# Regrouping the 64x64 products of a chunked recurrence into three runs, with ScalarE's order written out by hand

## The chip, the cores and the metric

One Trainium2 chip, one of its cores. The time is device time in microseconds (us) from launch to end, the median of several executions; lower is better. A profile is taken from one further execution of its own. The core has five instruction queues that run side by side and meet at semaphores: TensorE (PE in the profile; PEld is its weight load), VectorE (DVE), ScalarE (ACT), GpSimd (POOL) and SyncE (SP), which only issues DMAs here. GpSimd and ScalarE issue DMAs too.

## What is computed

Two blocks behind each other. The first is a recurrence over 768 tokens, for 4 batches x 8 heads with a 40x40 state each:

```python
for t in range(S):
    y[:, :, t] = np.einsum('bhd,bhde->bhe', rt, state)
    Sa = np.einsum('bhde,bhe->bhd', state, at)
    state_decay = state * wt[:, :, None, :] - np.einsum('bhd,bhe->bhde', Sa, bt)
    state = state_decay + np.einsum('bhd,bhe->bhde', vt, kt)
```

The second is a feed-forward block on the 3072 x 320 outcome:

```python
h = x @ w_in                                   # 320 -> 1024
e = np.exp(h - h.max(-1)); solu = h * e / (e.sum(-1) + 1e-9)
ln = (solu - mean(solu)) / np.sqrt(var(solu) + 1e-6) * g_ln
return ln @ w_out                              # 1024 -> 320
```

## The kernel before

The recurrence is worked off in chunks of 64 tokens, two batches at a time: 24 chunk pairs, numbered i, even and odd ones for the two batch pairs. Within a chunk the recurrence becomes matrix algebra with small products, one for each head: of 64x64 or less, 16 units to a step, that is 32 matmul instructions, since a product of float32 takes two. Four of them sit in the four quarters of TensorE's array. What the recurrence makes implicit is the inverse of a triangular 64x64 matrix for each head. The two 32x32 diagonal blocks of two chunks' heads are inverted together on VectorE (`invert`), the coupling of the blocks on TensorE (`couple`, `close`).

One pass of the main loop (line 785), called a slot here, does a bit of everything in a software pipeline. With i the slot's number, it solves and reads chunk i, prepares chunk i+1, makes decays and norms for chunk j = i+5, and does the feed-forward of chunks i-3 and i-4 (`m-2`, `m-3` with m = i-1). The stages, by the names of the tiles in the profile:

- `decay(i)` (L310): Ln of w on ScalarE (`lw`), a running sum on TensorE (`pcum`), two Exp (`ei`, `inv`). `decay_turned`: transposes `pei`, copied to `ex` by ScalarE.
- `front(i)`: transposes `pa` and `pb`; VectorE makes `aT`, ScalarE copies `bT`. `scaled` makes `kb` on GpSimd.
- `norm(i)`: products `pnt`, masked by VectorE into `nt` (L362), stored to DRAM (`nt_dram`, L388).
- `invert(n)` (L402): n counts pairs of chunks. `spread` loads the blocks back with four DMAs (`blk`, L399), then come 30 steps of VectorE, each a product and a subtraction (L415, L417); the first step begins with memsets (L407) and reads `blk` (L409). The outcome goes to `uu_dram`, from where `bring(i)` loads `tu` and `uh` on SP for each chunk.
- `flip`, `couple`: VectorE transposes `tu`, TensorE makes `py`, ScalarE copies it to `wy`. `close`: `pz`, copied into `tu`.
- `attend_kv`, `attend_rs`: transposes `pk`, `pv`, `pr` and of the state `pst`, copied by ScalarE to `kT`, `vT`, `rT`, `s`. `by_value` copies v and r on GpSimd for them. `scores`: products `ps` (two lots), masked to `psi` and `lv`.
- `carried`, `driven`: products `px`, copied to `x0`. `solved`: products `pu`, copied to `nuT` and `lu`. `answered`: `pl`, masked into `lu`.
- `read(i, own)`: `pyo`, outputs and state update, in two halves with a fence (a drain of TensorE) between. `leave(i)`: VectorE makes `x` (L604) and `tot` (L619) of it, GpSimd the new state; SP, and `left` on GpSimd, move `x` to `xT`.
- `hidden` (`h`, two matmuls of 512 columns each for full width, and two of half the rows), `exped` (maximum on VectorE, L655, Exp on ScalarE, L658), `weighed` (L664), `spreadof` (statistics, then a power on GpSimd, `rs`, L681), `folded` (transposes `plnT`), `output` (`po`, 16 matmuls in two lots, then `osb` and its store).

In the first slots `narrow` also converts the 64-bit weights, on VectorE and ScalarE, and `mean_begun` and `centred` take the mean out of the output weights.

The order of TensorE, VectorE, GpSimd and SP is the program's order, written by hand (line 87). ScalarE's order is left to the scheduler. The inverse is a Python generator: `some(n)` takes n steps off a list of begun inverses, and goes on in the next when one is used up. Where the steps stand between the other VectorE work is set by the four numbers of `shares`/`pieces` in each slot. An inverse is begun, and its `blk` loads issued, in slots where j is odd, so in even slots.

PSUM is used through three pools: `ps1` with two tiles of two banks each (`banks`: px, pu, pnt, pl, ps, py, pz, pyo in turn, eight in a slot), `ps2` with one tile of two banks (`h`), and `ps3` with two tiles of one bank (`bank`: transposes, pcum, po). A tile of a pool is used again when all readers of its last contents are done.

Of the kernel before, what the change touches and what calls it, by code (L numbers as in the profile page):

```python
# [48 lines left out]
def kernel(  # L49
# [37 lines left out]
    ctx.enter_context(tc.manual_schedule(engines={mybir.EngineType.PE, mybir.EngineType.Pool,  # L87
                                                 mybir.EngineType.DVE, mybir.EngineType.SP}))
# [85 lines left out]
    def split(dst, bits, c):  # L174
        n, width = dst.shape
        word = bits.bitcast(I32).rearrange("p (n two) -> p n two", two=2)
        hi, low16 = word[:, :, 1], bits.bitcast(U16).rearrange("p (n four) -> p n four", four=4)[:, :, 1]
        scale = two.tile([P, 512], I32, tag="scale", name="scale", bufs=1)[0:n, 0:width]
        ts, act, stt = nc.vector.tensor_scalar, nc.scalar.activation, nc.vector.scalar_tensor_tensor
        man = dst.bitcast(I32)  # L180

        ts(out=scale, in0=hi, scalar1=20, scalar2=0x7FF, op0=ALU.logical_shift_right, op1=ALU.bitwise_and)
        ts(out=man, in0=hi, scalar1=0xFFFFF, scalar2=None, op0=ALU.bitwise_and)
        act(out=scale, in_=scale, func=AF.Relu, scale=-1.0, bias=top[:, 0:1])
        act(out=scale, in_=scale, func=AF.Relu, scale=-2.0 ** 23, bias=top[:, 1:2])
        if c is None:
            g36 = 2.0 ** -36
            act(out=dst, in_=man, func=AF.Copy, scale=2.0 ** -20, bias=1.0)
        else:
            g, g20, g36 = (x[:, c:c + 1] for x in g_cols)  # L190
            act(out=dst, in_=man, func=AF.Identity, scale=g20, bias=g)
        yield
        stt(out=hi, in0=hi, scalar=-2 ** 31, in1=scale, op0=ALU.bitwise_and, op1=ALU.bitwise_or)
        stt(out=dst, in0=low16, scalar=g36, in1=dst, op0=ALU.mult, op1=ALU.add)
        nc.vector.tensor_tensor(out=dst, in0=dst, in1=hi.bitcast(FP32), op=ALU.mult)

    def narrow(n, n_steps=0):

        for x in range(n):
            load, part = next(parts)  # L200
            rest = split(*part)
            next(rest)
            some(n_steps // n + (x < n_steps % n))
            for _ in rest:
                pass

            if part is landed[load][-1] and load in LANDS_NEXT:
                land(LANDS_NEXT[load], nc.gpsimd)
        if not n:
            some(n_steps)  # L210
# [42 lines left out]
    def mm(o, lhsT, rhs, start=True, stop=True):  # L253
        nc.tensor.matmul(o, lhsT=lhsT, rhs=rhs, start=start, stop=stop, skip_group_check=True)  # L254

# [53 lines left out]

    def decay(i):  # L310
        if not ok(i):
            return
        d = st[i]
        lw = two.tile([P, DM], FP32, tag="lw", name="lw", bufs=1)
        nc.scalar.activation(out=lw, in_=d["raw_w"].rearrange("p h d -> p (h d)"), func=AF.Ln)
        t = (bank("pcum") if i > 5 else ps2.tile([P, DFF], FP32, tag="h", name="h"))[:, 0:DM]
        nc.tensor.matmul(t, lhsT=c_("cum"), rhs=lw, start=True, stop=True)
        nc.scalar.activation(out=ei_t[0][:, :, 0:D], in_=heads(t), func=AF.Exp)
        inv = d["inv"] = two.tile([P, DM], FP32, tag="inv", name="inv", bufs=4)
        nc.scalar.activation(out=inv, in_=t, func=AF.Exp, scale=-1.0)  # L320
# [31 lines left out]
    def front(i):  # L352
        if not ok(i):
            return
        d = st[i]
        t = turned("a", d["raw_a"])
        aT = d["aT"] = tokens("aT", AHEAD)
        nc.vector.tensor_tensor(out=aT[0:W2], in0=t, in1=d["ex"][0:W2, :, :, 0:C], op=ALU.mult)
        d["bT"] = kept("bT", turned("b", d["kb"][:, H:]))
# [33 lines left out]
    def spread(n):  # L393
        nb = two.tile([P, Q, Q], FP32, tag="blk", name="blk")
        for y in range(2):
            for e in range(2):
                home = C * y + Q * e
                queue = nc.gpsimd if n > 1 or y and not n else nc.sync
                queue.dma_start(out=nb[home:home + Q], in_=blocks[n][:, Q * e:Q * e + Q, Q * e:Q * e + Q])  # L399
# [77 lines left out]
    def attend_rs(i):  # L477
# [4 lines left out]
        d["rT"] = kept("rT", turned("r", r_t[0]), 2)  # L482
        if ci:
# [4 lines left out]
            d["s"] = two.tile([P, 4, P], FP32, tag="s", name="s")  # L488
# [36 lines left out]
    def driven(i):  # L525
# [3 lines left out]
        if d["opened"]:  # L529
            fence()  # L530
# [38 lines left out]
    def read(i, own):  # L569
# [14 lines left out]
        else:  # L584
            fence()
# [52 lines left out]
    def hidden(i, some):  # L638
# [4 lines left out]
        for kt, x in some:  # L643
            if (kt, x) == (0, 0):
# [3 lines left out]
               start=kt == 0, stop=kt == NK - 1)  # L648

    def exped(i):  # L650
# [3 lines left out]
        nmax = small.tile([P, 1], FP32, tag="nmax", name="nmax")  # L654
        nc.vector.tensor_reduce(out=nmax, in_=d["h"], axis=AX.X, op=ALU.max, negate=True)  # L655
        e = d["e"] = two.tile([P, DFF], FP32, tag="e", name="e", bufs=1)
        d["esum"] = small.tile([P, 1], FP32, tag="esum", name="esum")
        nc.scalar.activation(out=e, in_=d["h"], func=AF.Exp, bias=nmax, accum_out=d["esum"])  # L658
# [74 lines left out]
    for n in range(3):  # L733
        land(n, nc.sync)
    decay(0)
    decay_turned(0)
    for i in range(4):
# [4 lines left out]
        front(i)  # L742
        decay(i + 1)
        norm(i)
        decay_turned(i + 1)
        if i == 0:
            load_keys(2, "ba")
        if i == 1:
# [5 lines left out]
            load_keys(4, "w")  # L754
            some(8)
        if i == 2:
            load_values(0)
            load_keys(1, "k")
            some(8)
    load_keys(5, "w")  # L760
    load_keys(4, "ba")
    begin_inverse(1)
    for i in (2, 3):
        load_keys(i, "k", nc.gpsimd)
    by_value(0)
    scaled(2, "k")
    load_keys(4, "k", nc.gpsimd)
    scaled(3, "k")
    scaled(4)
    decay(5)  # L770
    load_keys(6, "w")
    land(3, nc.sync)
    some(14)
    load_keys(5, "ba")
# [3 lines left out]
    load_keys(5, "k")  # L778
    for n in (4, len(lands)):
        land(n, nc.sync)  # L780


    shares = {-1: (0, 6, 2, 6), 0: (0, 6, 4, 6), 1: (0, 6, 3, 6), 2: (0, 6, 3, 6), 3: (0, 6, 3, 6)}
    narrowed = {-1: (0, 1), 0: (1, 1), 1: (1, 2), 2: (1, 2), 3: (1, 1)}
    for i in range(-1, N + 3 + LAG):
        j, m = i + AHEAD, i - LAG
        pieces = shares.get(i, (3, 6, 0, 6))
        some_weights = narrowed.get(i, (0, 0))

        some(pieces[0])  # L790
# [4 lines left out]
        carried(i)  # L795
        driven(i)
        front(j)
        hidden(m - 2, ((0, 1),))
        if i == 3 + LAG:
            centred(mean, 6)  # L800
        load_keys(j + 3, "w")
        load_keys(j + 2, "bak")
        narrow(some_weights[0], pieces[1])

        solved(i)
        attend_kv(i + 1)
        hidden(m - 2, ((1, 1),))
        norm(j)
        attend_rs(i + 1)
        hidden(m - 2, ((2, 0), (2, 1)))  # L810
        exped(m - 2)
        decay_turned(j + 1)
        scaled(j + 1)
        left(i - 1)

        answered(i)
        if i >= 0:
            flip(i + 1)
        weighed(m - 2)
        spreadof(m - 2)  # L820
        decay(j + 2)
# [4 lines left out]
        output(m - 3, 0)  # L826
        if ok(j) and j % GRP == GRP - 1:
            begin_inverse(j // GRP)
        some(pieces[2])
        scores(i + 1)  # L830
        if i < 0:
            flip(i + 1)
        couple(i + 1)
# [4 lines left out]
        read(i, True)  # L838
        read(i, False)
        by_value(i + 2)  # L840
        leave(i)
        folded(m - 2)
        hidden(m - 1, ((0, 0), (1, 0)))
# [30 lines left out]
```

## Time and profile before

| | us |
|---|---|
| median of 3 executions | 639.46 (639.08 to 639.59) |
| the profiled execution, as timed | 639.79 |
| its span, first to last instruction | 637.7 |
| start of pu in slots 0, 1, 2, 3, 4 | 73.91, 94.70, 116.82, 139.74, 167.29 |
| in slots 14, 15, 16 | 393.72, 416.21, 438.69 |
| in slots 18, 20, 23 | 483.12, 523.46, 582.82 |

The starts of pu, the first product of `solved`, tell the slots apart: from slot 5 to slot 17 they are 22.48 us apart; from 18 on, where there are no chunks left to prepare, about 19.8; behind slot 23 comes a tail with the feed-forward of the last chunks alone. Times in the trace's views count from the start of the span. In a timeline each line is a group of like instructions: start, length, engine, line of the program, operation, tile written, tile read, count, and in brackets how long the engine sat idle before it and what released it. In a table of stretches the columns are the stretch, its length, each engine's busy time with the number of instructions, TensorE's granted clock as a share of full speed, and the DMA's share and rate.

### The profile page before, as it was taken

How to read it: one execution, taken by the hardware profiler on the slowest of the kernel's cores; microseconds unless marked ns; L12 is line 12 of the kernel's file. 1: busy time of each engine (PE TensorE's matmuls, PEld its weight loads, DVE VectorE, ACT ScalarE, POOL GpSimd, SP SyncE). 2: the span in 40 equal slices, each digit the busy share in tenths (PEclk: the TensorE clock that was granted, in tenths of full speed). 3: DMA queues.
4: the chain of work that ended last, by engine and by line, in shares of the span. 5: the costliest groups of instructions: out<-in, count | busy, mean ns of one | idle time of the engine just before them, and what ended most of it. 6: DMA issues, size and time to landing. Idle time of an engine off the chain costs nothing.

```text
span 637.7 us, 26729 instructions
## 1 busy us (share of the span) xinstructions
PE 567.5 (89%) x11451; PEld 399.6 (63%) x11451; DVE 461.9 (72%) x1286; ACT 245.3 (38%) x498; POOL 269.1 (42%) x444
## 2 busy tenths in 40 slices
PE   5245677988999999999999999999999999999995
PEld 3134555756577677667667767666776666766653
DVE  4678799999878778778878777787887796443431
ACT  3412545554334434433443443344243333332221
POOL 3334345574274444445543642743544642222200
PEclk9665676688999999999999999999999999999998
DMA  8939896474355535544554553654423422210000
GB/s 166 159 73 169 170 164 131 107 152 87 71 110 93 111 87 95 107 93 103 103 120 79 108 116 73 119 107 95 91 53 70 98 49 49 51 36 26 24 20 21
DMA packets 217868, 59.92 MB, mean 94 GB/s; under 512 B 203216, under 2 KB 213048, under 8 KB 217752
## 3 DMA queue, kind: packets, MB, share of 16 engines
q1 hardware_dynamic: 200984, 34.47, 31.7%
q0 software_dynamic: 11376, 19.25, 12.6%
q10 hardware_dynamic: 5392, 4.51, 2.5%
q8 instruction: 90, 1.47, 1.0%
q14 instruction: 26, 0.21, 0.1%
HBM read 40.10 MB, written 13.37 MB: 84 GB/s over the span
## 4 chain that ended last, share of the span: by engine, by line
PE 71%; DVE 13%; DMA 6%; issue 4%; ACT 2%; SPq 2%; POOL 1%; DVEq 0%; ACTq 0%; POOLq 0%
PE h L254 16%; PE po L703 14%; PE pyo L254 7%; PE px L254 4%; PE pu L254 3%; DVE uu L417 3%; PE plnT L692 3%; PE ps L254 3%; DVE prod L415 3%; PE pl L254 2%; PE pr L334 2%; PE pnt L254 2%; PE pk L334 2%; PE pa L334 2%; PE pz L254 2%
## 5 line engine op out<-in xcount | busy, mean ns | idle before, releaser
L254 PE MATMUL h<-w_in,xT 128*128 128x512 f32 (+1 forms) x288 | 121.6, 614 | 0.0
L415 DVE TENSOR_TENSOR prod<-blk,uu 128x30 f32<-128x30 f32 (+4 forms) x360 | 99.0, 275 | 24.0 <-DMA blk<-nt_dram 14.0
L703 PE MATMUL po<-w,lnT 128*128 128x320 f32 x384 | 113.5, 440 | 0.0
L417 DVE TENSOR_TENSOR uu<-uu,prod 128x30 f32<-128x30 f32 (+4 forms) x360 | 101.9, 283 | 12.4
L703 PEld LDWEIGHTS po<-w,lnT 128*128 128x128 f32 x384 | 70.5, 190 | 29.3 <-issue 2.3
L655 DVE TENSOR_REDUCE nmax<-h 128x1 f32<-128x1024 f32 x24 | 29.4, 1224 | 60.0 <-PE h L254 59.9
L388 POOL DMA_DIRECT2D nt_dram<-nt x20 | 18.3, 916 | 119.0 <-DVE nt L362 97.7
L254 PEld LDWEIGHTS h<-w_in,xT 128*128 128x128 f32 (+1 forms) x288 | 38.9, 190 | 21.9 <-issue 20.8
L623 POOL TENSOR_TENSOR st<-tot,ex 104x160 f32<-104x160 f32 x44 | 22.1, 520 | 70.4 <-DVE tot L619 68.2
L681 POOL TENSOR_TENSOR rs<-c,mhalf 128x1 f32<-128x1 f32 x24 | 13.4, 559 | 91.0 <-DVE c L680 89.6
L635 POOL DMA_DIRECT2D xT<-x x96 | 48.7, 512 | 0.0
L254 PE MATMUL pyo<-lv,kb 64*64 64x104 f32 x768 | 38.6, 274 | 6.0 <-DVE lv L362 3.3
L693 ACT COPY lnT<-plnT 128x512 f32<-128x512 f32 x48 | 26.1, 589 | 43.3 <-PE plnT L692 43.3
L399 POOL DMA_DIRECT2D blk<-nt_dram x42 | 33.3, 800 | 13.0 <-DMA nt_dram<-nt 12.7
L658 ACT ACTIVATE e<-h,nmax 128x1024 f32<-128x1024 f32 x24 | 26.8, 1115 | 28.6 <-DVE nmax L655 27.5
L254 PE MATMUL pyo<-lu,kb 64*64 64x104 f32 x768 | 37.2, 266 | 0.0
L664 DVE TENSOR_TENSOR e<-h,e 128x1024 f32<-128x1024 f32 x24 | 29.4, 1225 | 10.1 <-ACT e L658 10.1
L276 POOL DMA_DIRECT2D raw_r<-in_r_dram x48 | 34.9, 729 | 0.3 <-issue 0.3
L672 DVE BATCH_NORM_STATS2 bs<-e 128x6 f32<-128x512 f32 x48 | 30.9, 686 | 0.8
L707 ACT ACTIVATE osb<-po,rs 128x320 f32<-128x320 f32 x24 | 12.7, 528 | 48.5 <-PE po L703 29.6
L254 PEld LDWEIGHTS pnt<-aT,bT 40*64 40x64 f32 x768 | 14.6, 144 | 26.5 <-issue 25.0
L254 PEld LDWEIGHTS pyo<-lv,kb 64*64 64x64 f32 x768 | 23.9, 145 | 11.3 <-issue 7.7
(130 smaller groups left out, 1127.0 us busy)
## 6 DMA issues: line engine op xcount, KB each, us to landing
blk<-nt_dram POOLq DMA_DIRECT2D x42, 128.0 KB, 4.2
nt_dram<-nt POOLq DMA_DIRECT2D x20, 256.0 KB, 3.5
raw_w<-in_w_dram SPq DMA_DIRECT2D x48, 80.0 KB
a<-in_a_dram SPq DMA_DIRECT2D x48, 80.0 KB
raw_r<-in_r_dram POOLq DMA_DIRECT2D x48, 80.0 KB, 3.3
lv<-in_v_dram SPq DMA_DIRECT2D x48, 80.0 KB
out_dram<-osb ACTq DMA_DIRECT2D x24, 160.0 KB
raw_b<-in_b_dram SPq DMA_DIRECT2D x44, 80.0 KB
```

The costliest lines, as they stand in the source:

```text
L254: nc.tensor.matmul(o, lhsT=lhsT, rhs=rhs, start=start, stop=stop, skip_group_check=True)
L276: queue.dma_start(out=x[half(p), :, 0:D], in_=ap[2 * bp + p, :, ci * C:(ci + 1) * C, :].rearrange("h t d -> t h d"))
L334: nc.tensor.transpose(out=t[0:W2, j * P:(j + 1) * P], in_=x[:, 2 * j:2 * j + 2].rearrange("p a b -> p (a b)")[:, 0:W2], identity=ident)
L399: queue.dma_start(out=nb[home:home + Q], in_=blocks[n][:, Q * e:Q * e + Q, Q * e:Q * e + Q])
L415: nc.vector.tensor_tensor(out=t, in0=nb[:, j:j + 1, j + 1:Q].to_broadcast([P, n_c, m]), in1=u[:, 0:n_c, j:j + 1].to_broadcast([P, n_c, m]) ...
L417: nc.vector.tensor_tensor(out=u[:, 0:n_c, j + 1:Q], in0=u[:, 0:n_c, j + 1:Q], in1=t, op=ALU.subtract)
L635: nc.gpsimd.dma_start(out=xT[to:to + Q, 2], in_=x[at + P - 3 * D:at + D, 2])
L655: nc.vector.tensor_reduce(out=nmax, in_=d["h"], axis=AX.X, op=ALU.max, negate=True)
L658: nc.scalar.activation(out=e, in_=d["h"], func=AF.Exp, bias=nmax, accum_out=d["esum"])
L664: nc.vector.tensor_tensor(out=d["e"], in0=d["h"], in1=d["e"], op=ALU.mult)
L672: nc.vector.bn_stats(out=bs[:, x], in_=d["e"][:, x * 512:x * 512 + 512])
L703: nc.tensor.matmul(d["out"][:, 0:DM], lhsT=d["lnT"][:, f, :], rhs=w2[:, f, :], start=f == 0, stop=f == NF - 1)
```

## The change

TensorE's order in a slot is rearranged so that steps of 64x64 products stand together: pu and ps; py, pnt and pl; pz, pyo, px, half-width h, pyo and px. `carried` and `driven` of chunk i+1 move to the end of slot i, `scores` to the beginning of a slot, the transposes of k, v, r one slot earlier, behind `folded`. Two fences become one. The tile h is begun with its half-width products. ScalarE's order is now the program's too, with `couple` ahead of `exped`, whose maximum becomes a step of its own (`highest`); Ln of decay is a function of its own (`logged`), called early in the prologue alone. The shares of inverse steps are new, and most of them stand behind the masks of `scores` and `norm`. In the prologue the first norms' stores stand ahead of some loads on SP, two weight conversions overlap in `narrow`, with two buffers for `scale`, and `s` has one buffer for two.

```diff
-    ctx.enter_context(tc.manual_schedule(engines={mybir.EngineType.PE, mybir.EngineType.Pool,
-                                                 mybir.EngineType.DVE, mybir.EngineType.SP}))
+    ctx.enter_context(tc.manual_schedule(engines={mybir.EngineType.PE, mybir.EngineType.Pool, mybir.EngineType.DVE,
+                                                 mybir.EngineType.SP, mybir.EngineType.Activation}))
...
     def narrow(n, n_steps=0):
+        begun = []
         for x in range(n):
             load, part = next(parts)
-            rest = split(*part)
-            next(rest)
-            some(n_steps // n + (x < n_steps % n))
+            begun.append((load, part, split(*part)))
+            next(begun[-1][-1])
+        some(n_steps)
+        for load, part, rest in begun:
...
+    def logged(i):
+        lw = st[i]["lw"] = two.tile([P, DM], FP32, tag="lw", name="lw", bufs=1)
+        nc.scalar.activation(out=lw, in_=st[i]["raw_w"].rearrange("p h d -> p (h d)"), func=AF.Ln)
...
-            if (kt, x) == (0, 0):
+            if (kt, x) == (NK - 1, 0):
                 d["h"] = ps2.tile([P, DFF], FP32, tag="h", name="h")
...
-    for n in range(3):
+    for n in range(2):
         land(n, nc.sync)
+    load_keys(2, "ba")
     decay(0)
+    logged(1)
...
     by_value(0)
+    begin_inverse(1)
+    attend_kv(0)
+    attend_r(0)
     scaled(2, "k")
...
+    some(10)
+    scores(0)
     decay(5)
...
-    shares = {-1: (0, 6, 2, 6), 0: (0, 6, 4, 6), 1: (0, 6, 3, 6), 2: (0, 6, 3, 6), 3: (0, 6, 3, 6)}
-    narrowed = {-1: (0, 1), 0: (1, 1), 1: (1, 2), 2: (1, 2), 3: (1, 1)}
+    shares = {-1: (0, 10, 2, 2), 0: (4, 5, 3, 4), 1: (0, 6, 4, 5), 2: (4, 4, 3, 4), 3: (0, 6, 4, 5)}
+    narrowed = {-1: (1, 0), 0: (1, 1), 1: (1, 2), 2: (1, 2), 3: (1, 1)}
     for i in range(-1, N + 3 + LAG):
         j, m = i + AHEAD, i - LAG
-        pieces = shares.get(i, (3, 6, 0, 6))
+        pieces = shares.get(i, (0, 5, 4, 4) if i % GRP else (3, 5, 4, 5))
```

The new slot, from the loop's head to its end, with `front` split into `front` (a) and `front_b` (b), and `attend_rs` into `attend_r` and `stated`:

```python
if i >= 1: bring(i + 1)
if i >= 0: load_values(i + 2)
some(pieces[0])
solved(i)
if i >= 0: scores(i + 1)
load_keys(j + 3, "w"); load_keys(j + 2, "bak")
stated(i); front(j); hidden(m - 2, ((0, 1),))
narrow(some_weights[0], pieces[1])
front_b(j); decay_turned(j + 1); hidden(m - 2, ((1, 1),))
flip(i + 1); highest(m - 2); by_value(i + 2); scaled(j + 1); left(i - 1)
decay(j + 2)
if i == 3 + LAG: centred(mean, 6)
output(m - 3, 0)
some(pieces[2])
couple(i + 1); exped(m - 2); norm(j); answered(i); weighed(m - 2); spreadof(m - 2)
if ok(j) and j % GRP == GRP - 1: begin_inverse(j // GRP)
...
output(m - 3, 1)
narrow(some_weights[1], pieces[3])
close(i + 1); read(i, True); carried(i + 1)
if ok(m - 1): hidden(m - 1, ((2, 0), (2, 1)))
fence()
read(i, False); driven(i + 1); leave(i); folded(m - 2)
hidden(m - 1, ((0, 0),)); attend_kv(i + 2); hidden(m - 1, ((1, 0),)); attend_r(i + 2)
```

## The prediction, made before the changed kernel was run

> **What bounds the kernel now.** I read the page's summary first, then the matmul starts of one pass of the main loop, then the queues of VectorE and GpSimd around the inverse.
>
> ```profile
> PE 567.5 (89%) x11451; PEld 399.6 (63%) x11451; DVE 461.9 (72%) x1286; ACT 245.3 (38%) x498; POOL 269.1 (42%) x444
> PEclk9665676688999999999999999999999999999998
> PE 71%; DVE 13%; DMA 6%; issue 4%; ACT 2%; SPq 2%; POOL 1%; DVEq 0%; ACTq 0%; POOLq 0%
> ```
> ```profile
> core 0: us, PE busy (x) PEld busy (x) DVE busy (x) ACT busy (x) POOL busy (x), PEclk, DMA share, GB/s
> 236.34:461.18 224.84, 222.63 (x4822) 157.00 (x4821) 175.04 (x501) 92.39 (x189) 109.92 (x180) 1.00 0.50 100
> ```
>
> The second block is ten slots (a slot is one pass of the main loop): TensorE is busy 222.6 of 224.8 us at full clock, so a slot is its list of matmuls, 22.48 us, and nobody is waited for. VectorE has 17.5 us of work in it. From here T=0 is the start of a slot's first pu product; pu of slots 4 and 20 start at 167.29 and 523.46 in the timeline.
>
> ```profile
> 394.80 0.65 PE L334 MATMUL pk<-cst,kb 128*104 128x128 f32 x4
> 395.28 0.60 PE L334 MATMUL pv<-cst,v 128*104 128x128 f32 x4
> 395.72 1.02 PE L254 MATMUL h<-w_in,xT 128*128 128x512 f32 x2
> 396.67 0.69 PE L254 MATMUL pnt<-aT,bT 40*64 40x64 f32 x32
> 397.30 0.64 PE L334 MATMUL pr<-cst,r 128*104 128x128 f32 x4
> ...
> 403.46 0.69 PE L254 MATMUL ps<-aT,kT 40*64 40x64 f32 x32
> 403.97 0.65 PE L254 MATMUL ps<-rT,vT 40*64 40x64 f32 x32
> 404.44 0.62 PE L254 MATMUL py<-tu,nt 64*64 64x32 f32 x32
> ```
>
> Start to start, 32 small products take 0.47 us inside a run (403.97 to 404.44), 0.63 alone (pnt). The wide step ahead pays too: four h take 1.81 up to px and two 0.95 up to pnt, so two more cost 0.86 and the exit 0.09; eight po take 2.25 or 2.35, while sixteen in the tail with no small product behind take 4.41 (599.05 to 603.46), half of that being 2.2; the first transpose behind takes 0.48 for 0.44. One entry and exit thus costs about 0.16+0.1+0.04 = 0.3 us.
>
> ```profile
> 398.42 0.91 POOL L388 DMA_DIRECT2D nt_dram<-nt  x1 [6.85 <-DMA lv<-in_v_dram]
> 405.29 0.56 POOL L681 TENSOR_TENSOR rs<-c,mhalf 128x1 f32<-128x1 f32 x1 [1.22 <-DVE c L680]
> 406.10 3.15 POOL L399 DMA_DIRECT2D blk<-nt_dram  x4 [0.25 <-issue]
> ```
> ```profile
> 410.33 0.76 DVE L604 TENSOR_TENSOR x<-pyo,ex 104x256 f32<-104x256 f32 x2 [0.58 <-PE pyo L254]
> 411.01 0.55 DVE L619 TENSOR_TENSOR tot<-pyo,st 104x160 f32<-104x160 f32 x2
> 411.72 0.48 DVE L407 MEMSET uu<- 64x512 f32 x1 [0.16 <-issue]
> ...
> 414.40 0.19 DVE L415 TENSOR_TENSOR prod<-blk,uu 128x30 f32<-128x30 f32 x1 [1.46 <-DMA blk<-nt_dram]
> ```
>
> These two show an inverse's birth in slot 14: the norm goes to DRAM, rs, then four blk loads until 409.25, which VectorE awaits until 414.40, 5.15 us later. The new inverse's first instruction (411.72) stands **behind** the x and tot of leave, so this wait delays nobody who frees PSUM.
>
> [...] after 2.37 us without a matmul the clock is 0.52 for 3.5 us.
>
> ```profile
> 153.50:155.70 2.20, 0.00 (x0) 0.00 (x0) 2.13 (x6) 0.00 (x0) 0.30 (x1) 1.00 0.06 9
> 155.70:159.20 3.50, 3.32 (x84) 3.01 (x88) 3.19 (x13) 1.81 (x4) 0.00 (x0) 0.52 0.02 5
> ```
>
> [...] In the trace memset, blk wait and the work behind stand in program order.
>
> **The change part by part.** *Runs of small products.* Before there are seven (px; pu; pnt; half-width h; pl; ps and py; pz and pyo), after three (pu, ps / py, pnt, pl / pz, pyo, px, half h, pyo, px). Four entries fewer: 4 x 0.3 = 1.2 us a slot. [...] One fence of two goes: px before a fence takes 0.79 instead of 0.51, 0.28 us. Slot: 22.48-1.48 = 21.0.
>
> *ScalarE by hand.* Ln of decay now stands behind ex instead of a slot early (402.51 in the trace). pei to ex takes 0.74, the next ScalarE instruction starts 0.47 later, Ln 0.48: 1.69; TensorE has pei 0.46 and one h pair 0.86 meanwhile, so pcum waits 0.4 us. pl reuses py's bank, and needs wy: 0.69 from py to wy, 0.47 for it, against 0.98 for py and pnt: 0.25 us. Bounds for both: 0 if the copies start earlier than that, 1.2 in sum if each waits behind another copy. Slot: **21.65, a gain of 0.8**. Exp behind wy is hidden: it ends near T+11 and weighed comes at T+11.5 on VectorE. h is allocated earlier, before the fence at T+16; weighed ends at T+12.7. One buffer for s costs nothing, its reader is a slot back.
>
> *Inverse steps, the dear part.* An inverse has 30 counted steps; `some` finishes one generator and goes on in the next without asking. Before, shares sum to 15 in each slot from 1 on, and each inverse ends with an even slot. After, slots 1 to 3 still have 15 each, but from slot 4 on even ones have 3+5+4+5 = 17 and odd ones 13. Steps of inverse 3 in slot 4: 16-18, 19-23, 24-27, and in the last share 28-30 **and steps 1 and 2 of inverse 4**, begun moments ago in the same slot. So in slots 4, 6, ... 18, eight times, memset and blk wait now stand **ahead** of leave on VectorE.
>
> When does blk land? TensorE: pu and ps 2.0 (0.51, 2 x 0.47, 0.56), pst 0.53, pa, pb, pei 0.44 each, two h pairs 0.86 each to 5.6, the wait 0.4 and pcum 0.55 to 6.5, po to 8.8, py and pnt to 9.75. Mask of nt until 10.9, lu 11.5, weighed 12.7 (1.23), two statistics to 14.05, four small ones to 14.8. GpSimd: lv is issued on SP 7.7 us behind the start of leave's x (388.00 to 395.68 in the timeline), which is now at T-4.4; with some 3 us of landing (raw_r's is 3.3) T+6.1, then the copies of v and r 0.9, kb 2 x 0.87, six xT issues 3.1, the norm's store at T+11.8; its landing takes 3.5, T+15.3. rs at 14.9 to 15.5, then blk 15.7 to 18.85, and with 4.2 (page) to 5.15 us of landing, **T+23.0 to 24.0**. VectorE stands there since T+16.6. Then the rest of two steps (0.9), x and tot (1.3): T+25.2 to 26.2. These free pyo's bank pair; with two pairs in turn and eight allocations a slot, pu of the next slot needs just that pair. It would have started at T+21.65. TensorE idles 3.7 to 4.7 us, say **4.3**, and restarts at half clock for some 3.5 us, losing **1.8**. Bounds: 2.5 and no clock loss; 6 and 2.5. Queued behind the wait: leave, its xT stores on SP, and behind these bring and lv of the next slot, 3 us later; flip then needs tu near T+6.5 and gets it about then.
>
> *Prologue and early slots.* nt of chunk 1 is stored at 20.02, though masked at 17.44, because loads of chunk 2 stand ahead on SP; moved, blk lands some 2.4 us sooner. narrow overlaps two conversions with a second scale buffer. bring(0) (SP at 65.20) no longer stands behind raw_b and a. I take 3 us up to slot 0. Slots 0 to 3 are VectorE's (85.2 of 93.4 us busy); scores at the slot's front end waits for the lv mask (8 waits, 15.3 us in all): 4 us, floor 0, ceiling 8. In slot 4 centred now stands before po, which waits for its two subtractions: 2 us back. Sum -5, between -10 and +3.
>
> **Sum**, against the profiled execution, 639.8 us (span 637.7 and 2.1 around it; 0.3 above the median): early -5; slots 4 to 19, 16 x 0.85 = -13.6; eight stalls of 4.3+1.8 = +48.8; slots 20 to 23 -3.4; the tail has wide matmuls alone, 0. Forecast 639.8+26.8 = **666.6, 666 on the median's scale**.
>
> **Rivals.** (a) The stall comes, but the clock stays up: 8 x 1.8 less, **652**. For it: in slot 4 a gap of 1.42 us (170.43) left the clock at 1.00. Against: 2.37 did not. (b) The blk wait never reaches TensorE, and the whole regrouping counts: 639.8-5-13.6-3.4 = **618**. This is the other side; it decides where blk lands before T+19.3, since 2.2 us of VectorE work still have to fit before T+21.65. For it: landings of 3.3 and 3.5 us, the shortest in the trace, give T+20. Against: rs holds GpSimd until 15.5 and the issues alone take 3.15. (c) Landing is as slow as the slowest seen (6.9) [...]: 3 us more a time, **690**. (d) Stall and gain cancel: 640.
>
> **How the numbers follow.** Forecast 0.60, (a) 0.14, (b) 0.11, (c) 0.12, (d) 0.03. About 0.2%, 1.3 us, is what a measurement can tell from no change. Faster 0.12, same 0.02, slower 0.86. The forecast's own range is 650 to 684; with most of (a) and (c) 640 to 690.
>
> **What would show it.** Right: from slot 4 on, pu starts in pairs, one gap of about 21.7 and one of 28 us, idle TensorE before pu put down to tot; L407 ahead of L604 in even slots, L415 waiting some 7 us for blk; PEclk dented every second slot. Regrouping right: ps behind pu at 0.47 a piece, three entries. Wrong: even spacing below 22 us, or blk landing before leave's products are done.

## The result, and the profile after

The changed kernel takes **684.75 us** (median of 4 executions, 683.75 to 685.29), the kernel before beside it 639.53 (639.08 to 640.11): a ratio of **1.0705, 95% interval 1.0686 to 1.0723**. The forecast was 666, with 640 to 690 as the range and 0.86 for slower. The profiled execution has a span of 683.2 us, 45.5 more than before. A ratio is taken over the faster executions of each kernel alone and a median over all of them, so that the two need not agree to the last digit where executions scatter.

The page's lines on busy time, on the granted clock in 40 slices, and on the chain that ended last, for the changed kernel:

```profile
PE 571.0 (84%) x11451; PEld 409.2 (60%) x11451; DVE 460.4 (67%) x1286; ACT 248.8 (36%) x498; POOL 269.5 (39%) x448
PEclk9555675678999999999999998999989999999998
PE 46%; DVE 19%; DMA 16%; POOL 7%; SPq 4%; issue 4%; ACT 3%; DVEq 0%; ACTq 0%; POOLq 0%
```

TensorE has as many instructions as before and about the same busy time; what grew is time in which it stands. The chain has lost its owner: TensorE's share fell from 71% to 46%, while VectorE's, DMA's and GpSimd's rose from 13, 6 and 1% to 19, 16 and 7%. The waits on the way of the inverse's blocks have grown most clearly, VectorE's for their loads and GpSimd's for the store ahead of these (columns: total us, times, longest):

```profile
DVE uu L419 <- DMA blk<-nt_dram: 50.9, 9, 8.9
POOL blk L409 <- DMA nt_dram<-nt: 39.4, 9, 8.3
```

Before, VectorE waited for `blk` 14.0 us in all and GpSimd for `nt_dram` 12.7.

The starts of pu divide the loss. The last column is the kernel after with the overrun taken out (first experiment below), that is, without the steps of a new inverse that stand ahead of leave; all in us of the profiled executions.

| stretch | before | after | predicted change | measured change | without overrun |
|---|---|---|---|---|---|
| span's start to pu of slot 4 | 167.29 | 177.90 | -5 | +10.6 | 172.43 |
| pu of slot 4 to pu of slot 20 | 356.2 | 394.9 | +35.2 | +38.7 | 374.8 |
| pu of slot 20 to the end | 114.2 | 110.4 | -3.4 | -3.8 | 110.6 |

The middle and the end went nearly as predicted; the early slots are wrong in sign.

**An undisturbed slot.** TensorE's timeline in slot 8, whose pu starts at 280.54 and the next at 302.56 (start, length, operation, and the wait ahead of it):

```profile
285.22 1.02 PE L254 MATMUL h<-w_in,xT 128*128 128x512 f32 x2
286.48 0.81 PE L322 MATMUL pcum<-lw,cst 128*128 128x320 f32 x2 [0.24 <-ACT lw L313]
...
289.86 0.68 PE L254 MATMUL pnt<-aT,bT 40*64 40x64 f32 x32
290.64 0.69 PE L254 MATMUL pl<-rT,nuT 40*64 40x64 f32 x32
...
295.36 0.68 PE L254 MATMUL px<-st,aT 40*64 40x40 f32 x32
295.96 1.13 PE L254 MATMUL h<-w_in,xT 64*128 64x512 f32 x4
297.18 0.41 PE L254 MATMUL pyo<-lv,kb 64*64 64x104 f32 x8
```

The slot takes 22.02 us, 0.46 less than before. pcum starts 1.26 behind the h pair, which without a wait takes 0.86 (283.49 to 284.35 for the same pair): 0.40 lost to lw. pl starts 0.78 behind pnt where 0.47 is the pace: 0.31. Half-width h within the third run takes 0.60 to enter and 1.22 to pass; before, between full-width steps, 0.53 and 1.06. In the new order the fence that is left stands behind it, so its own price can't be read apart.

**A slot with an overrun.** VectorE's timeline at the end of slot 6 and in the beginning of slot 7:

```profile
247.41 0.48 DVE L417 MEMSET uu<- 64x512 f32 x1 [0.17 <-issue]
...
256.63 0.42 DVE L419 TENSOR_SCALAR uu<-blk 64x512 f32<-64x512 f32 x1 [8.58 <-DMA blk<-nt_dram]
...
258.48 0.76 DVE L614 TENSOR_TENSOR x<-pyo,ex 104x256 f32<-104x256 f32 x2 [0.19 <-issue]
...
260.81 0.68 DVE L363 TENSOR_TENSOR aT<-pa,ex 104x512 f32<-104x512 f32 x1
```

GpSimd's, which made it late:

```profile
239.14 0.45 POOL L308 COPY v<-lv 128x320 f32<-128x320 f32 x1 [6.92 <-DMA lv<-in_v_dram]
...
244.68 0.92 POOL L398 DMA_DIRECT2D nt_dram<-nt  x1
...
251.16 3.17 POOL L409 DMA_DIRECT2D blk<-nt_dram  x4 [4.51 <-DMA nt_dram<-nt]
```

And TensorE's, with the two windows around its longer stop (start and end, length, busy us of PE, PEld, DVE, ACT and POOL, then clock, DMA share, GB/s):

```profile
254.07 0.69 PE L254 MATMUL ps<-aT,kT 40*64 40x64 f32 x32 [1.04 <-ACT lu L567]
...
256.94 0.60 PE L339 MATMUL pb<-cst,kb 128*104 128x128 f32 x4
261.54 0.80 PE L339 MATMUL pei<-cst,ei 128*104 128x128 f32 x4 [4.00 <-DVE aT L363]
```
```profile
257.40:261.50 4.10, 0.14 (x2) 0.00 (x0) 3.78 (x12) 0.59 (x1) 1.88 (x4) 1.00 0.05 15
261.50:265.00 3.50, 3.46 (x9) 1.98 (x10) 2.49 (x11) 0.95 (x2) 0.35 (x1) 0.56 0.50 107
```

The memset of the new inverse stands ahead of x, and VectorE then waits 8.58 us for blk. All through this the next slot's pu (251.88), ps, pst, pa, h and pb run: TensorE does not stop at pu. It stops twice behind it. The short stop is at ps, which waits 1.04 us until ScalarE has copied pu's product (`lu`). This wait stands in each of the slots 5, 7, ... 19, eight times, 8.4 us in all, and neither in the kernel without the overrun nor in the one with the two steps behind leave; that ps has to take over pu's pair of banks, because a late leave still holds the other pair, is the reading that fits. The long stop is at pei, for aT, which empties the bank of pa. aT waits in VectorE's queue behind the inverse, x, tot and the masks of ps. Then come 4.1 us without work and 3.5 us at clock 0.56. Shorter stops could cost pace too: behind one of 2.23 us (ScalarE's order in the old slot) po takes 3.97 us in place of 2.32.

### The profile page after: what moved, and what is told of

Its sections match the earlier page's. It is cut to its first block, busy times and chain, and to the rows that moved or that the text cites. A ratio compares the mean times of both kernels' runs of the same rounds, so it can differ in the third digit from the quotient of the medians.

```text
span 683.2 us, 26641 instructions
## 1 busy us (share of the span) xinstructions
PE 571.0 (84%) x11451; PEld 409.2 (60%) x11451; DVE 460.4 (67%) x1286; ACT 248.8 (36%) x498; POOL 269.5 (39%) x448
## 3 DMA queue, kind: packets, MB, share of 16 engines
q0 software_dynamic: 11568, 19.78, 12.4%
## 4 chain that ended last, share of the span: by engine, by line
PE 46%; DVE 19%; DMA 16%; POOL 7%; SPq 4%; issue 4%; ACT 3%; DVEq 0%; ACTq 0%; POOLq 0%
PE h L254 10%; PE po L718 9%; DMA blk<-nt_dram 5%; PE pyo L254 5%; DVE uu L427 5%; DMA nt_dram<-nt 5%; DVE prod L425 4%; PE pu L254 3%; POOL blk L409 3%; PE px L254 3%; PE plnT L707 2%; PE ps L254 2%; DMA raw_b<-in_b_dram 2%; POOL xT L645 2%; POOL kb L334 1%
## 5 line engine op out<-in xcount | busy, mean ns | idle before, releaser
L254 PE MATMUL h<-w_in,xT 128*128 128x512 f32 (+1 forms) x288 | 127.5, 630 | 0.0
L718 PE MATMUL po<-w,lnT 128*128 128x320 f32 x384 | 117.0, 451 | 3.5 <-DVE w L233 3.0
L427 DVE TENSOR_TENSOR uu<-uu,prod 128x30 f32<-128x30 f32 (+4 forms) x360 | 107.8, 300 | 12.4
L308 POOL COPY v<-lv 128x320 f32<-128x320 f32 x24 | 11.4, 475 | 122.6 <-DMA lv<-in_v_dram 97.7
L665 DVE TENSOR_REDUCE nmax<-h 128x1 f32<-128x1024 f32 x24 | 28.6, 1193 | 18.6 <-PE h L254 18.6
L549 ACT COPY x<-px 128x320 f32<-128x320 f32 x24 | 10.2, 426 | 81.5 <-PE px L254 81.5
L419 DVE TENSOR_SCALAR uu<-blk 64x512 f32<-64x512 f32 x12 | 5.2, 434 | 51.0 <-DMA blk<-nt_dram 50.9
L464 ACT ACTIVATE wy<-py,cst 128x256 f32<-128x256 f32 x24 | 11.4, 474 | 76.1 <-PE py L254 76.1
L372 DVE TENSOR_TENSOR psi<-ps,cst 128x512 f32<-128x512 f32 x24 | 16.5, 687 | 33.3 <-PE ps L254 33.3
L614 DVE TENSOR_TENSOR x<-pyo,ex 104x256 f32<-104x256 f32 x48 | 18.1, 419 | 30.2 <-PE pyo L254 11.0
L254 PEld LDWEIGHTS pyo<-lv,kb 64*64 64x64 f32 x768 | 23.9, 144 | 21.5 <-issue 21.5
L277 POOL DMA_DIRECT2D raw_r<-in_r_dram x48 | 33.9, 710 | 0.0
L339 PE MATMUL pei<-cst,ei 128*104 128x128 f32 x96 | 17.9, 318 | 19.1 <-DVE aT L363 18.5
```

The costliest lines, as they stand in the source:

```text
L277: queue.dma_start(out=x[half(p), :, 0:D], in_=ap[2 * bp + p, :, ci * C:(ci + 1) * C, :].rearrange("h t d -> t h d"))
L339: nc.tensor.transpose(out=t[0:W2, j * P:(j + 1) * P], in_=x[:, 2 * j:2 * j + 2].rearrange("p a b -> p (a b)")[:, 0:W2], identity=ident)
L372: nc.vector.tensor_tensor(out=dst, in0=t.rearrange("p b (j c) -> p b j c", j=4), in1=tri.unsqueeze(1).unsqueeze(1).to_broadcast([P, 2, 4, ...
L427: nc.vector.tensor_tensor(out=u[:, 0:n_c, j + 1:Q], in0=u[:, 0:n_c, j + 1:Q], in1=t, op=ALU.subtract)
L614: nc.vector.tensor_tensor(out=x[0:W2, 2 * q:2 * q + 2].rearrange("p g (b t) -> p b g t", b=2), in0=y[:, q, :, 0:C].rearrange("p (b g) c -> ...
L718: nc.tensor.matmul(d["out"][:, 0:DM], lhsT=d["lnT"][:, f, :], rhs=w2[:, f, :], start=f == 0, stop=f == NF - 1)
```

## The experiments

Twelve kernels ran. "After" and "before" name the kernel that a diff starts from; it is after where nothing else is said. Ratios are to the kernel before on the same chip.

### Without the overrun

```diff
-    shares = {... 3: (0, 6, 4, 5)}
+    shares = {... 3: (0, 5, 4, 4)}
```

Two steps fewer in slot 3 keep the inverses apart: steps 1 and 2 of the new one fall into the next slot.

> The changed kernel with slot 3 given 13 inverse steps for 15, so that each inverse ends with the last share of an even slot and no step of the next one stands ahead of leave there. Theory A (the blk wait ahead of leave is what slots 4 to 19 lose): even spacing of pu at about 22.0 us from slot 6 on, the gaps of 28 us gone, time 635 to 645. Theory B (the regrouping or ScalarE's written order makes the slots long, and the wait for blk merely moves to the next slot's first share): above 665.

Measured: 659.09 us, ratio 1.0232 (1.0161 to 1.0303). This is between the two. The gaps of some 28.6 us are gone, so the overrun is a cause, and the largest one found: 25.7 of 45 us by the medians, though the four executions scatter from 650.75 to 660.65. In the profiled executions 20.1 of these fall into slots 4 to 19. Most of the 5.5 ahead of slot 4 is chance: pu of slot 3, up to which both kernels run the same instructions, starts at 143.52 here and at 148.36 in the changed kernel. But slots 6 to 19 average 22.9 us, for 22.1 before, and pu of slot 6 starts at 227.1 against 213.86 before: a second cause sits ahead of it. A third appears in TensorE's timeline of slot 15, in the middle of a run, without anything to wait for:

```profile
433.99 0.91 PE L254 MATMUL ps<-rT,vT 40*64 40x64 f32 x20 [2.99 <-issue]
```

There are five such stops, in slots 5, 10, 11, 15 and 19, 9.8 us in all; the kernel before has none. Behind the three longest (1.90, 2.99 and 3.08 us) the clock is 0.50 to 0.54 for 3.5 us (the 20 products shown take 0.91 us; with the conversions moved, 19 of them behind a stop in the same slot take 0.56), which by an estimate from these figures costs some 5 us more: together the greater part of what the middle still loses.

### The overrun alone, in the old order

From before, with two steps more in slot 3:

```diff
-    shares = {... 3: (0, 6, 3, 6)}
+    shares = {... 3: (0, 6, 3, 8)}
```

> The kernel before with 17 inverse steps in slot 3 for 15, so that from slot 4 on every even slot does two steps of the inverse just begun ahead of leave, as the changed kernel does. If the overrun costs some 6 us a time wherever it stands: 685 to 690. If its price comes from how late blk lands in the new order (in the old one 20.7 us behind pu, and about 5 us of matmuls can go ahead of the next product that needs VectorE): 640 to 650.

Measured: 652.32, ratio 1.0199 (1.0179 to 1.022), 12.5 us more than the kernel before on its chip. That is just above the second range and far from the first. VectorE's timeline of slot 4:

```profile
185.83 0.48 DVE L407 MEMSET uu<- 64x512 f32 x1 [0.17 <-issue]
...
187.62 0.42 DVE L409 TENSOR_SCALAR uu<-blk 64x512 f32<-64x512 f32 x1 [1.16 <-DMA blk<-nt_dram]
...
191.86 0.19 DVE L415 TENSOR_TENSOR prod<-blk,uu 128x30 f32<-128x30 f32 x1 [3.67 <-DMA blk<-nt_dram]
```

The same two steps at the same place cost 1.6 us each of the eight times, where taking them out of the new order gains 3.2 by the medians and 2.5 by slots 4 to 19 of the profiled executions. In the old order the waits are 1.16 and 3.67 us and not 8.58: the norm is stored 5 to 7 us behind the start of pu there, and not 12 to 17. The same fault has a price that goes with the slot it stands in.

### The two steps behind leave

```diff
-        pieces = shares.get(i, (0, 5, 4, 4) if i % GRP else (3, 5, 4, 5))
+        pieces = shares.get(i, (0, 5, 4, 4) if i % GRP else (3, 5, 4, 3))
...
         leave(i)
+        if i > 3 and i % GRP == 0:
+            some(2)
```

> The changed kernel with the two steps of the new inverse moved behind leave in the even slots from 4 on. If leave's PSUM is what TensorE waits for, as predicted (pu of the next slot): 635 to 645, like the run without the overrun. If it is the rest of VectorE's queue, above all aT, which holds the bank that pei needs: leave alone is freed, 1.3 us a time, so 670 to 678, and TensorE still stops before pei.

Measured: 665.92, ratio 1.0431 (1.0368 to 1.0495). Neither number: by the medians the steps behind leave gain 19 of the 26 us. In the profiled executions, though, slots 4 to 19 take 375.5 us here and 374.8 without the overrun, so that in this stretch the place behind leave gains nearly all; most of the other difference stands ahead of slot 3, where the instructions are the same. VectorE's wait for blk falls from 50.9 to 26.4 us, mostly since it begins later in the slot, as blk's last part lands only 0.7 us earlier on the mean of the eight (T+25.9 for T+26.6, from the start T of the slot's pu). TensorE's wait at ps is gone, and the one at pei for aT falls from 18.5 to 7.6, since aT still stands behind the inverse. A loop, in which a late leave makes the next inverse later still, is not shown: in slots 8 to 18 of the changed kernel blk lands at T+27.0, 24.3, 27.8, 23.4, 28.7 and 23.9, late and early by turns.

### ScalarE's written order in the old slot

```diff
-                                                 mybir.EngineType.DVE, mybir.EngineType.SP}))
+                                                 mybir.EngineType.DVE, mybir.EngineType.SP, mybir.EngineType.Activation}))
```

From before. Its ScalarE instructions run in the order in which the program names them, and nothing else is changed.

> The kernel before with ScalarE in the program's order and nothing else. There exp (which waits for the maximum until some 6 us behind pnt) stands ahead of ex and Ln, so pcum comes some 2 us later in each slot with a decay: 670 to 690 if that is on the path, as TensorE's order is. If ScalarE has enough slack (38% busy) for any order: 640 to 645.

Measured: 686.39, ratio 1.0748 (1.0727 to 1.0769): as expected. TensorE's timeline:

```profile
439.35 0.88 PE L317 MATMUL pcum<-lw,cst 128*128 128x320 f32 x2 [2.23 <-ACT lw L315]
440.02 3.97 PE L703 MATMUL po<-w,lnT 128*128 128x320 f32 x8
```

Ln stands behind ex, pcum waits 2.23 us (33.9 us in all, 17 times), and po takes 3.97 where 2.32 is usual. Of the thirteen such waits of 2.23 or 2.24 us from 180.30 to 492.23, eight are followed by a po of 3.62 to 4.00 us and five by one of 2.32. In the new slot h pairs stand between pei and pcum and the same wait is 0.24.

### Three ways to give ScalarE another order in the new slot

All three start from the kernel without the overrun. The first leaves ScalarE to the scheduler again:

```diff
-                                                 mybir.EngineType.SP, mybir.EngineType.Activation}))
+                                                 mybir.EngineType.SP}))
```

The second takes Ln a slot early:

```diff
         exped(m - 2)
+        if ok(j + 3):
+            logged(j + 3)
```

> The run without the overrun (659.1 us, pu of slot 6 at 227.1), with ScalarE's order left to the scheduler again. If ScalarE's written order is what the early slots lose (the conversions of narrow ahead of bT, ex, Ln and the copy into tu, so that pcum, py and px wait): pu of slot 6 before 220 and 645 to 652 in all. If the early loss comes from the new order of TensorE and its lower clock: 656 to 662.

> The run without the overrun, and Ln of decay of chunk j+3 behind exped in the slot ahead, so that pcum finds its input. The profile of the changed kernel shows pcum waiting 0.4 us in an undisturbed slot and 1.7 to 3.0 us in slots 0 to 3. If these waits are on the path: 18 x 0.4 and some 8 us of the early slots less than the run without the overrun, so 622 to 632. If another wait takes their place: within 3 us of it.

Measured: 680.88, ratio 1.063 (1.0568 to 1.0693), and 670.46, 1.0443 (1.0372 to 1.0514). Both missed. With the early Ln the profiled execution, the shortest of its four, takes only 364.6 us from slot 4 to slot 20; the loss stands ahead of it. With the scheduler, py waits for tu 27.8 us and pl for wy 20.1: the written order is worth some 22 us in this slot, and is not what makes the early slots long (pu of slot 6 at 228.5). With Ln early the undisturbed slots are 21.5 to 21.7 us, the 0.4 us of pcum's wait, but in the prologue Ln then waits for raw_w with ScalarE's whole queue behind it: pu of slot 0 at 80.92 in place of 70.87.

A third takes Ln early from slot 4 on only, with the moved conversions of the next section:

```diff
         exped(m - 2)
+        if i > 3 and ok(j + 3):
+            logged(j + 3)
```

> The run with narrow behind, and from slot 4 on Ln of the next slot's decay behind exped, so that pcum doesn't wait. An undisturbed slot goes from 22.0 to 21.6 us, so some 5 us less than the run with narrow behind; if the pauses of TensorE for other reasons set the time, no difference over 3 us.

Measured: 661.27, ratio 1.0302 (1.0262 to 1.0342), a miss: slots of 21.5 to 21.8 where nothing disturbs, but slots 9, 13, 15 and 17 at 26 to 27. In 13 and 17 VectorE meets blk unlanded at the new inverse's first steps (1.66 us in slot 13), flip comes late, py waits 1.5 and 2.4, and po behind it takes 4.63 us in both, where 2.42 is usual. So a slot quicker by 0.4 us can use up the inverse's slack. In 9 and 15 it is stops within a run of ps, 2.14 and 2.44 us, and pst behind them takes 1.09 in both, where 0.65 is usual.

### The early slots

From the kernel without the overrun, the conversions of the weights (`narrow`) are moved behind decay and behind close, and `centred` goes back behind the first h pair (its lines are left out here):

```diff
-        narrow(some_weights[0], pieces[1])
+        some(pieces[1])
...
         decay(j + 2)
+        narrow(some_weights[0])
...
-        narrow(some_weights[1], pieces[3])
+        some(pieces[3])
         close(i + 1)
+        narrow(some_weights[1])
```

> The run without the overrun, with ScalarE's order still written, but narrow's conversions behind decay and behind the copy into tu, and centred right behind the first h pair as before the change. If the places of these are what slots 0 to 5 lose: the waits of pcum for lw in slots 0 to 3 fall from 2.7 to under 1 us, po's wait of 3.2 us in slot 4 goes, 642 to 650. If VectorE's load bounds these slots whatever the order: within 4 us of 659.

Measured: 657.15, ratio 1.0249 (1.0217 to 1.0281), pu of slot 6 at 227.8: the second. In slot 0 TensorE stands 3.43 us before pz for the mask nt. VectorE's timeline of slot 1 without the overrun had shown a loop:

```profile
93.35 0.69 DVE L372 TENSOR_TENSOR psi<-ps,cst 128x512 f32<-128x512 f32 x1 [2.52 <-PE ps L254]
...
106.08 0.68 DVE L372 TENSOR_TENSOR nt<-pnt,cst 128x512 f32<-128x512 f32 x1
```

From psi to nt is VectorE's stretch, 12.7 us; from nt over pz, pyo and px to the next ps is TensorE's, at the end of which VectorE waits for ps again (1.33 us, psi at 119.50). The next experiment starts from this last kernel and empties VectorE's stretch:

```diff
-    shares = {..., 0: (4, 5, 3, 4), 1: (0, 6, 4, 5), 2: (4, 4, 3, 4), 3: (0, 5, 4, 4)}
+    shares = {..., 0: (7, 2, 1, 6), 1: (0, 4, 3, 8), 2: (7, 2, 1, 5), 3: (0, 4, 2, 7)}
...
-        narrow(some_weights[0])
         output(m - 3, 0)
...
         spreadof(m - 2)
+        narrow(some_weights[0])
```

> The variant with narrow behind decay and close (median 657 us, pu of slot 6 at 227.8 us), and in slots 0 to 3 inverse steps and conversions taken out of the stretch of VectorE between the mask of ps (psi) and the mask of pnt (nt): shares (7,2,1,6), (0,4,3,8), (7,2,1,5), (0,4,2,7) in place of (4,5,3,4), (0,6,4,5), (4,4,3,4), (0,5,4,4), and the first conversions behind spreadof. Theory: what makes slots 0 to 3 of the new order long is a loop, pu and ps, psi on VectorE, all that VectorE does up to nt, then pz to the next ps on TensorE (about 10 us), in which VectorE's stretch takes 13 us and TensorE stands before py and pz; so work moved out of the stretch shortens each slot by 2 to 4 us, pu of slot 6 starts at 212 to 220 us and the time is 641 to 651 us. Rival: the place in the slot doesn't matter, since VectorE's sum of work or the loads set these slots; then pu of slot 6 stays within 3 us of 227.8 and the time within 4 us of 657.

Measured: 657.23 us, ratio 1.0228 (1.0179 to 1.0276); pu of slot 6 at 226.2 (in the profiled execution, at 666.79 us the longest of the four). By the numbers the theory missed, and the rival's came. TensorE's timeline at the end of slot 0:

```profile
94.37 1.06 PE L339 MATMUL pr<-cst,r 128*104 128x128 f32 x4 [5.42 <-ACT kT L348]
```

And ScalarE's, where the copy kT follows at 93.64:

```profile
91.43 0.72 ACT L184 ACTIVATE scale<-scale,top 128x512 int32<-128x512 int32 x1 [5.17 <-DVE scale L182]
```

The stops before pz are down from 3.43, 3.00 and 3.11 us in slots 0, 1 and 2 to none, 1.21 and none. In their place TensorE stands before pr, 5.42 and 5.03 us in two slots of this one execution: kT is queued on ScalarE behind a conversion that waits for its first half on VectorE, now late. So the place does matter, and what was gained at one was lost at another. That each conversion crosses from VectorE to ScalarE and back, in two queues written by hand, is shown; whether a place exists at which it holds up neither was not tried.

### The stops within a run

128 drains at the head of TensorE's stream, else the kernel without the overrun; they shift the position of every later instruction.

```diff
+    for _ in range(128):
+        nc.tensor.drain()
```

> The run without the overrun, with 128 drains at the head of TensorE's stream, where it idles for 6 us. Without the overrun TensorE stops five times in the midst of a run of ps or pb for 0.8 to 3.1 us with nothing to wait for, 9.8 us in all. If these stops are instruction fetches that come late [...]: they leave the slots 5, 10, 11, 15 and 19 or change length, and turn up in other slots[...]. If they come from what the DMA engines carry at that time in the slot alone: the same slots, the same lengths within 0.5 us.

Measured: 658.44, ratio 1.0258 (1.0219 to 1.0298). TensorE's timeline in slot 13:

```profile
387.31 0.63 PE L256 MATMUL ps<-rT,vT 40*64 40x64 f32 x27
390.31 0.34 PE L256 MATMUL ps<-rT,vT 40*64 40x64 f32 x5 [2.37 <-issue]
```

The stops are in slots 0, 8, 13, 17 and 18 now. They go with the place in the stream of instructions; and in four other kernels with this order of TensorE (the steps behind leave; the conversions moved; the same with Ln early from slot 4 on; the front of the slot emptied) the stop of slot 5 stands ahead of the same last nine products of ps. The page counts 90 packets of instructions of 16 KB, about one for each 254 of TensorE's 22,902 matmuls and weight loads. Whose packets they are it does not tell. That a stop is a late fetch is the reading that fits; no run removed the fetches.

### Joining products in the old order

Two edits of before: the norm's products right behind pu, and then half-width h right ahead of pl as well, with decay_turned (pei) ahead of it.

```diff
         solved(i)
+        norm(j)
         attend_kv(i + 1)
         hidden(m - 2, ((1, 1),))
-        norm(j)
         attend_rs(i + 1)
```

> The kernel before with one step moved: norm right behind solved, so that pnt follows pu in one run of 64x64 products, six runs a slot for seven, and everything else as it was. If joining two runs is worth the 0.3 us read from the trace and no wait follows: 22.2 us a slot, 5 to 7 us in all, 632 to 635. If VectorE's nt mask, now ahead by a step, or bT makes TensorE wait instead: 639 or more.

```diff
         attend_rs(i + 1)
+        decay_turned(j + 1)
         hidden(m - 2, ((2, 0), (2, 1)))
         exped(m - 2)
-        decay_turned(j + 1)
         scaled(j + 1)
```

> The run with norm joined, and the half-width h behind pei, so that it stands right ahead of pl. If the change between 64x128 and 64x64 is cheaper than two changes to full width: another 0.1 to 0.3 us a slot, 2 to 6 us less than that run. If any change of the tiling costs the same: within 1.5 us of it.

Measured: the first **636.1 us (635.47 to 637.28, 6 executions), ratio 0.9954 (0.9941 to 0.9967)**, faster than both kernels of this study and a little short of the 632 to 635 expected. An undisturbed slot is 22.21 us in place of 22.48. Its TensorE timeline:

```profile
392.15 0.67 PE L254 MATMUL pnt<-aT,bT 40*64 40x64 f32 x32
392.75 0.64 PE L334 MATMUL pk<-cst,kb 128*104 128x128 f32 x4
```

pnt stands behind pu (second lot at 391.71, 0.44 ahead) in the same run, and pk follows 0.60 later: one entry and exit less, 0.27 us. The second is 642.2, ratio 1.005 (1.0033 to 1.0068), a miss by 6 us: pei, now close behind the transposes, waits 0.24 for rT's copy, 15 times, and half-width h ahead of pl takes 1.06 as before, so that next to nothing was gained by the joining: standing ahead of 64x64 products instead of full-width ones saved it nothing.

## Why the prediction was right, and where not

**Regrouping.** Four entries at 0.3 and a fence were to give 1.48 us a slot. With the two waits added to what the slot gained, 0.46 + 0.40 + 0.31, it gave 1.17. What is missing is one entry: half-width h is one of the seven runs counted before, and it still stands in the new slot, inside the third run. The sum's four entries count it among those saved. Three entries and the fence make 3 x 0.3 + 0.28 = 1.18, an estimate from the same figures. The unit price of 0.3 holds, the 0.27 of the joined norm confirms it on its own. Half-width h takes 1.06 us up to the next product both between full-width steps and, in the second joined kernel, ahead of 64x64 products.

**ScalarE.** pcum's wait was predicted at 0.4 and measured at 0.40, pl's at 0.25 and at 0.31. The experiments add what the sum didn't ask: the same order in the old slot costs 47 us, in the new one leaving it to the scheduler costs 22.

**The overrun.** That two steps of the new inverse would stand ahead of leave, eight times, was right. The landing of blk was mis-sized: predicted T+23.0 to 24.0, measured T+23.4 to 29.9, in slot 6 T+27.7. Two terms made it late: the norm's store at T+12 to 15.4 for T+11.8 (T+17.5 in slot 4, where it waits for the mask), and its landing, 5.3 us for 3.5, which GpSimd then waits for. Late leaves are only a small part of this: without the overrun the store is at T+11.6 to 14.2 from slot 6 on.

**The step that failed here** is "pu of the next slot needs just that pair". It does not: pu and what follows up to pb run on, about 5 us of cover but for the 1.04 us at ps, and the long stop comes at pei by way of VectorE's queue. The two errors nearly cancel where blk lands 4.9 us or more behind the next pu: slots 7, 9, 13 and 17 take 28.6 to 29.6 us, about 7 more than 22.0, with a stop of 3.8 to 4.5 us at pei and a clock of 0.50 to 0.67 behind it for 3.5 us, near the predicted 4.3 and 1.8. Where blk lands 1.3 to 3.3 us behind the next pu, slots 5, 11, 15 and 19, only 1.3 to 3.1 are lost. Measured against undisturbed slots the eight cost 37.6 us, for 48.8; taking the overrun out gives back no more than 20.1 of them, as the stops within a run then come in. The slot's smaller gain (0.46 for 0.85, over 16 slots 6 us) and slot 4, 28.5 us long where 24.1 was usual, use up that credit, so that the sum of the middle is near by luck, for partly wrong reasons.

**The early slots** are the term that made the forecast 18 us too low: -5 predicted, +10.6 measured up to slot 4, against 3.5 us of error in the middle. The size of that loss is uncertain: with the same instructions pu of slot 3 starts at 148.36, 147.24 and 143.52 in three profiled executions of the new order, and at 139.74 and 141.24 in two of the old one. Only the gain of the prologue came (pu of slot 0 at 72.15, 1.8 earlier, for 3). "Slots 0 to 3 are VectorE's (85.2 of 93.4 us busy)" holds for the old order only. The same window of the changed kernel, pu of slot 0 to pu of slot 4:

```profile
72.15:177.90 105.75, 76.74 (x1722) 59.69 (x1722) 82.47 (x228) 44.47 (x92) 43.79 (x71) 0.73 0.56 108
```

VectorE has less to do than before (82.5 us) and is idle for 23; TensorE's busy time is 76.7 us for 75.5, but the window is 12.4 longer, and the clock 0.73 for 0.82. So the sum of work no longer sets these slots; the round between the engines does. TensorE's stops there are before pcum for lw (10.1 us in four slots), py for tu (7.4), pz for nt (4.7) and px for tu (3.8), waits of the engines for each other, where the sum had "4 us, floor 0, ceiling 8" of gain. The 15.3 us of waits for the lv mask that stood behind this gain count each wait twice, once for the matmul and once for its weight load: there are four, 7.4 us. The runs exclude ScalarE's written order and the place of the conversions each as the cause alone, and show stops that change place when work is moved. What the smallest set of moves is that gives these 12 us back stays open.

**Rivals.** (a), no loss of clock, is refuted by 0.56 in the window after the stop. But the length of a stop alone does not tell what the clock does behind it. In the kernel before, 1.43 us at pr in slot 2 (121.69) are followed by 0.51 for 3.5 us, where the prediction's 1.42 in slot 4 left 1.00; with the conversions moved, 2.72 us within ps in slot 5 (206.58) are followed by products at full pace (pst 0.65 us, the h pairs 1.02). (b), the other side, needed blk by T+19.3; it never came before T+23.4. (c), slow landing at 690, came nearest in time; in part it is what happened, by the store's landing. The 684.75 lie inside the wide range and just outside the forecast's own 650 to 684; with the early slots wrong in sign, that they lie so near is in part luck. That removing the overrun leaves 659 and not 618 shows that (b)'s sum was too bright also without the stall.

## What to carry to other kernels

When counted steps are dealt out over a pipeline, follow the count over the boundary to the next unit of work: two steps too many put a wait for a DMA ahead of the instructions that free the buffers and feed the queues of the next round. In a slot that is bound by one engine, a gain of tenths from joining small products is real, and the simplest move gets it (one line, 0.46% of the time); a full reordering has to bring along every engine that was only just in time. Where an engine has slack on average, ask for the round from its first wait to its last before its sum.

## What the runs showed of the hardware

- TensorE can stop within a run of matmuls without a wait, for 0.53 us (the changed kernel) to 3.08 us (without the overrun), at places that move with the instruction stream: slots 0, 8, 13, 17 and 18 with 128 drains ahead, for 5, 10, 11, 15 and 19. All five stops of the kernel without the overrun add up to 9.8 us; in the changed kernel itself the view of slots 5 to 19 shows one, of 0.53. Why it is spared was not tried.
- Behind a stop the clock was about half for some 3.5 us, or it was not: 0.51 behind 1.43 us and 1.00 behind 1.42 (both in the kernel before), 0.50 to 0.54 behind the three longest stops without the overrun, 0.56 behind the 4.00 at pei in the changed kernel, and full pace behind 2.72 with the conversions moved. What decides it these runs do not show.
- Half-width products (64*128 in the views), moved from between full-width steps to right ahead of 64x64 ones, take the same 1.06 us. Their price inside a run of small products was not measured apart from the fence behind them.
- In the changed kernel a store of 256 KB to DRAM lands 5.3 us after its issue in the median (3.5 before), and a load of 128 KB, of which four bring two such stores back, 4.9 (4.2 before): a round over DRAM of some 10 us and more, with the issues between them.
